# A recurrent attention and two-layer network kernel on one core: the first step and its network taken apart by batch, a new order of the first four steps, and one product that waits for the keys' transfers

## The chip, the core and the metric

The kernel runs on one core of a Trainium2 chip. The metric is the time of one execution on the device, in microseconds (us); less is better. The core has five engines with queues of their own: TensorE (PE; its weight loads are listed as PEld), VectorE (DVE), ScalarE (ACT), GpSimd (POOL) and SyncE (SP). SP, ACT and POOL also issue DMA transfers. An instruction waits on semaphores for what other engines or transfers must have done, and what stands behind it on its engine waits with it.

## What is computed

A gated recurrence over 768 positions (4 batches, 8 heads of 48), whose output is laid out as 3072 tokens of 384, and a two-layer network with a leaky activation:

```python
f = 1.0 / (1.0 + np.exp(-f_logit))
for t in range(S):
    state = f[:, :, t, :, None] * state + np.einsum('bhd,bhe->bhde', k[:, :, t], v[:, :, t])
    y[:, :, t] = np.einsum('bhd,bhde->bhe', q[:, :, t], state)
x = y.transpose(0, 2, 1, 3).reshape(B * S, H * D)
h = x @ w_in                                            # 384 -> 2048
g = np.maximum(h, 0.0) + alpha * np.minimum(h, 0.0)
out = g @ w_out                                         # 2048 -> 384
```

Inputs arrive in float32, the two weight matrices as 8-byte floats that the kernel turns into float32 itself.

## The kernel before

The work is cut into 12 steps: six chunks of 128 positions, and in each two pairs of batches (U = 2 batches a step, so 256 tokens). Steps 0 and 1 are the first chunk of the two pairs; they start from an empty state and use a shorter form of the diagonal blocks.

A step has four parts.

- *Preparation* (`prepare`, letter P, five pieces): loads of gates, queries, keys and values; the sigmoid on ScalarE; a chain of VectorE products that builds the decayed queries (`qd`, lags 1 to 3, lines 286 to 295), two scans of decays (317, 319), decayed keys (`k4`, `kh`, `ks`) and quads (`us`). From the second chunk on the keys are turned by VectorE (`kt`, line 401) and put in place by 16 small transfers from SP into `ksn` (line 427).
- *Carry* (`carry`, letter O, two pieces): the products between half chunks (`off`, line 444), in the first chunk also the half scores (454) and a turn of the keys by TensorE (`pk`, 471); then the new state (`pd`, line 484), which reads `ksn`, and its sum into `vs`.
- *Attention* (`attend`, letter S): for each batch raw scores (520) and quad scores (535), copied under masks into `ad` by VectorE; `ad` is copied by ScalarE into the score matrix `A` (563, eight copies of 32x256); the output product `py` (574), copied to `y`. Step 0 brings `y` into the layout `xT` by products with `dense` (592); the others do it by ten transfers on SP, ACT and POOL (603).
- *Network* (`network`, letter n): the first layer over 256 columns, eight tiles `ph` with two blocks of 128 hidden units each (618), a Relu on ScalarE (623), two gate instructions on VectorE (625). In step 0 the second layer is plain (`po`, 638). In the other steps it is seven half-size products `pa` to `pe` (657) with sums of gates (702).

The 16 weight pieces (letters a, w for the first matrix; b, v for the second) are loaded by SP into five raw buffers, converted by two ScalarE instructions each (224, 225), and put together by one VectorE instruction (234). W are differences of the second matrix that the seven products need.

The order of TensorE, VectorE and ScalarE is written out by hand as a string of these letters: `FIRST` for four steps, `USUAL` for every step from the fourth on. One letter runs one piece of a part, with all its instructions on all engines. POOL's and SP's instructions are placed by a scheduler. PSUM has two buffers of two banks (`psa`) for the attention and four single banks (`psn`) for the network. Before everything stand 52 small matmuls on constants (`idle`, line 736). In the usual order of TensorE a step reads: raw and quad of batch 0, first-layer tiles 0 and 1 of the step before, raw and quad of batch 1, tiles 2 and 3, off, state, tiles 4 to 7, pa, pb, output, pc, pd, pa, pc, pe.

Of the kernel before, what the change touches and what calls it, by code (L numbers as in the profile page):

```python
# [8 lines left out]
F32 = mybir.dt.float32  # L9
# [12 lines left out]
U = 2  # L22
# [4 lines left out]
IDLE = 52  # L27
# [3 lines left out]
FIRST = (  # L31
        "P5 a2 P a O w S w a w a2 S Q S O S w Q2 S Q2 S w",
        "a2 w2 n O b w n b2 S P v2 n2 S b v Q n b n O S2 v n b v n Q2 b v Q b n S v2 W Q W S n2 W n",
        "n S P n2 S W n W n O Q n3 O S Q n S Q n Q S2 Q n3",
        "S n3 P S Q S n O n O n4 Q S Q S Q n S Q n Q n2",
)
USUAL = "S n2 S n2 O2 n Q n3 Q n Q S3 n Q S n Q n Q n"

def flat(first, usual, steps=12):
    out = []  # L40
    left = {}
    for n in range(steps + 1):
        for key in (first[n] if n < len(first) else usual).split():
            for _ in range(int(key[1:] or 1)):
                k = key[0]
                if k in "awbvW":
                    out.append((k,))
                else:
                    m = n - 1 if k == "n" else n + 1 if k == "Q" else n
                    k = "P" if k == "Q" else k  # L50
                    if 0 <= m < steps:
                        out.append((k, m))
    return out

# [4 lines left out]
def kernel(  # L59
# [12 lines left out]

# [31 lines left out]
    psn = ctx.enter_context(tc.tile_pool(name="psn", bufs=4, space=bass.MemoryType.PSUM))  # L120

    def pair(name):
        return psa.tile([128, 2, 512], F32, tag="pair", name=name)

    def bank(name):
        return psn.tile([128, 512], F32, tag="net", name=name)
# [35 lines left out]
    nc.gpsimd.memset(mquad, 0.0)  # L162
    for m in range(1, NB):
        lo = UO[m] + (4 if m == 1 else 0)
        n = NB - m
        nc.gpsimd.tensor_copy(mquad[:, lo:lo + 4 * n].rearrange("p (i r) -> p i r", r=4),
                              inq[:, 0:n].unsqueeze(2).broadcast_to((128, n, 4)))
    mhalf = const.tile([128, VW], F32, tag="mhalf", name="mhalf")
    nc.gpsimd.memset(mhalf, 0.0)
    for half in range(2):  # L170
        for m in range(1, NQ):
            n = NQ - m
            lo = 16 * half + 4 if m == 1 else VO[m] + 4 * n * half
            nc.gpsimd.tensor_copy(mhalf[:, lo:lo + 4 * n].rearrange("p (i r) -> p i r", r=4),
                                  inq[:, NQ * half:NQ * half + n].unsqueeze(2).broadcast_to((128, n, 4)))
# [7 lines left out]
    make_identity(nc, ident)  # L183
    nc.gpsimd.tensor_scalar(om, om, -1.0, 1.0, ALU.mult, ALU.add)


    dense = work.tile([128, DM], F32, tag="o", name="dense")
    nc.gpsimd.memset(dense, 0.0)
    for par in range(2):
        nc.gpsimd.tensor_copy(dense[:, (2 + par) * D:(3 + par) * D], ident[:, 64 * par:64 * par + D])  # L190

    def load_weights(dst, src, name):

        rows_ = NK if dst is w_in_sb else 1
        pieces_ = dst.shape[1] * dst.shape[2] // WP
# [4 lines left out]
        got = {}  # L210

        def of(n):
            return dst[:, :, n * width:(n + 1) * width]
# [3 lines left out]

        def upper(n):
            raw = stage.tile([128, WP, 4], I16, tag="raw", name=f"{name}_raw{n}", bufs=RAWS)
            nc.sync.dma_start(out=raw.rearrange("p (a n) four -> p a (n four)", a=rows_)[:, :, 0:4 * width - 1],  # L220
                              in_=words[:, :, 4 * n * width + 1:4 * (n + 1) * width])

            lead = stage.tile([128, WP], F16, tag="lead", name=f"{name}_lead{n}", bufs=LEADS)
# [575 lines left out]
```

## Time and profile before

| What | Value |
|---|---|
| time, median of 3 runs | 621.4 us (621.33 to 623.4) |
| span of the profiled execution | 622.1 us |
| TensorE busy | 592.1 us, 95% |
| VectorE busy | 497.1 us, 80% |
| ScalarE busy | 246.6 us, 40% |
| POOL busy | 63.0 us, 10% |
| first-layer matmuls (L618) | 258.7 us in 1152 passes |

The profile shows one execution; its own time is known by its span alone, which is 0.7 us over the median of the runs. The span is cut there into 40 slices, with the busy share of each engine in tenths. Every float32 matmul shows as two passes, so a tile of six matmuls counts 12. Passes overlap: the mean of one is longer than the distance between the starts of two. The first real matmul starts at 17.8 us, the first-layer's first at 49.0 us, the first raw score of step 4 at 198.1 us; from there a step takes 47.7 us.

### The profile page before, as it was taken

To read this page: it belongs to the slowest core of one execution; us is meant where nothing else is said; L and a number is where in the kernel's file an instruction comes from. 1 tells how busy PE (TensorE), PEld (TensorE's weight loads), DVE (VectorE), ACT (ScalarE), POOL (GpSimd) and SP (SyncE) were. 2 spreads that over 40 slices of the span, in tenths; PEclk is the share of its full clock that TensorE was granted. 3 is DMA by queue.
4 is the path that set the end of the run, shared out by engine and by line. 5 is a ranking of instruction groups with operands and counts; after the bars stand their busy time and mean duration, and the time that the engine had idled before them with its cause. 6 is when DMAs were issued, how large, how long until landed. Compare 5 with 4: busy or idle time off the path is not lost.

```text
span 622.1 us, 19062 instructions
## 1 busy us (share of the span) xinstructions
PE 592.1 (95%) x8212; PEld 529.8 (85%) x8212; DVE 497.1 (80%) x997; ACT 246.6 (40%) x466; POOL 63.0 (10%) x117
## 2 busy tenths in 40 slices
PE   3568999999999999999999999999999999999997
PEld 3457866898899899899899899899889889889997
DVE  7588998899898798798798798798888888762261
ACT  5677862441641272262261351352253243223110
POOL 9120010001000011001001001001001000000000
PEclk9999999999999999999999999999999999999999
DMA  9964632014404314214313313413313401201000
GB/s 290 367 234 155 190 85 52 36 36 108 98 8 96 72 35 107 67 35 95 79 35 90 84 35 88 86 36 86 87 36 85 87 3 26 53 2 27 26 0 26
DMA packets 68116, 50.43 MB, mean 81 GB/s; under 512 B 47168, under 2 KB 60608, under 8 KB 68032
## 3 DMA queue, kind: packets, MB, share of 16 engines
q1 hardware_dynamic: 56656, 25.01, 15.6%
q0 software_dynamic: 6864, 22.35, 12.7%
q10 hardware_dynamic: 4512, 1.85, 1.7%
q8 instruction: 65, 1.06, 0.7%
q14 instruction: 19, 0.16, 0.1%
HBM read 36.21 MB, written 4.72 MB: 66 GB/s over the span
## 4 chain that ended last, share of the span: by engine, by line
PE 88%; DVE 6%; ACT 3%; issue 2%; DMA 1%; ACTq 0%; DVEq 0%
PE ph L618 39%; PE pc L657 9%; PE pa L657 8%; PE pd L657 5%; PE pe L657 4%; PE pb L657 4%; PE py L574 4%; PE po L638 3%; PE raw L520 3%; PE qu L535 3%; PE pd L484 3%; PE off L444 1%; PE xt L592 1%; DVE gate L625 1%; DMA f<-in_fT 1%
## 5 line engine op out<-in xcount | busy, mean ns | idle before, releaser
L618 PE MATMUL ph<-xT,w_in_sb 128*128 128x256 f32 x1152 | 258.7, 382 | 0.7 <-DVE Csum L661 0.7
L618 PEld LDWEIGHTS ph<-xT,w_in_sb 128*128 128x128 f32 x1152 | 216.4, 190 | 33.4 <-issue 2.3
L623 ACT ACTIVATE neg<-ph 128x512 f32<-128x512 f32 x96 | 57.4, 598 | 200.8 <-PE ph L618 139.5
L625 DVE SCALAR_TENSOR_TENSOR gate<-neg,om,ph 128x256 f32<-128x256 f32 x192 | 82.7, 478 | 50.6 <-ACT neg L623 50.4
L657 PE MATMUL pc<-t,S 128*128 128x192 f32 x352 | 61.7, 329 | 0.0
L657 PE MATMUL pa<-w_out_sb,gate 128*128 128x192 f32 x352 | 61.3, 327 | 0.1
L657 PEld LDWEIGHTS pa<-w_out_sb,gate 128*128 128x128 f32 x352 | 57.9, 190 | 1.0 <-DVE gate L625 0.4
L657 PEld LDWEIGHTS pc<-t,S 128*128 128x128 f32 x352 | 57.3, 190 | 0.6
L526 DVE COPY_PREDICATED ad<-mraw,raw 128x256 f32<-128x256 int32 (+1 forms) x96 | 42.4, 442 | 11.1 <-PE raw L520 8.6
L541 DVE COPY_PREDICATED ad<-mquad,qu 128x224 f32<-128x224 int32 (+6 forms) x140 | 42.0, 300 | 6.2
L419 ACT COPY A<-q 48x512 f32<-48x512 f32 x44 | 27.2, 619 | 36.1 <-DVE q L368 35.7
L563 ACT COPY A<-ad 32x256 f32<-32x256 f32 x96 | 38.7, 403 | 1.4
L330 DVE TENSOR_TENSOR us<-us,fs 128x768 f32<-128x768 f32 (+5 forms) x60 | 36.8, 614 | 0.0
L678 ACT ACTIVATE o<-pa 128x192 f32<-128x192 f32 x11 | 3.7, 332 | 75.2 <-PE pa L657 72.3
L661 DVE SCALAR_TENSOR_TENSOR Csum<-pc,Csum 128x192 f32<-128x192 f32 x22 | 7.9, 357 | 30.3 <-PE pc L657 30.1
L287 DVE TENSOR_TENSOR qd<-qd,f 128x768 f32<-128x768 f32 (+2 forms) x36 | 27.2, 756 | 6.0 <-ACT qd L282 6.0
L520 PEld LDWEIGHTS raw<-qd,k 48*32 48x32 f32 x1536 | 18.5, 109 | 15.3 <-issue 13.1
L520 PE MATMUL raw<-qd,k 48*32 48x80 f32 x1536 | 24.0, 243 | 7.6 <-issue 4.4
L702 DVE TENSOR_TENSOR S<-gate 128x512 f32<-128x512 f32 x44 | 30.3, 688 | 0.8
L657 PE MATMUL pe<-w_out_sb,S 128*128 128x192 f32 x176 | 30.4, 326 | 0.0
L657 PE MATMUL pd<-w_out_sb,S 128*128 128x192 f32 x176 | 30.4, 326 | 0.0
L657 PE MATMUL pb<-t,gate 128*128 128x192 f32 x176 | 30.4, 326 | 0.0
(101 smaller groups left out, 758.3 us busy)
## 6 DMA issues: line engine op xcount, KB each, us to landing
w_out_raw<-in_w_out SPq DMA_DIRECT2D x8, 767.8 KB, 5.8
w_in_raw<-in_w_in SPq DMA_DIRECT2D x8, 767.2 KB, 11.9
q<-in_qT POOLq DMA_DIRECT2D x11, 512.0 KB, 4.2
f<-in_fT POOLq DMA_DIRECT2D x11, 512.0 KB, 4.5
k<-in_kT POOLq DMA_DIRECT2D x11, 512.0 KB, 4.9
out<-o SPq DMA_DIRECT2D x24, 192.0 KB, 2.7
vs<-in_v POOLq DMA_DIRECT2D x22, 192.0 KB, 4.6
ksn<-kt SPq DMA_DIRECT2D x80, 32.0 KB, 2.0
```

Of the source, the lines that this page charges most:

```text
L287: nc.vector.tensor_tensor(qdv[d], qdv[d - 1][:, :, :, 1:5 - d], f[:, :, 1:5 - d].rearrange("p (g i) r -> p g i r", i=NB), ALU.mult)
L330: nc.vector.tensor_tensor(us[:, :, UO[m]:UO[m] + 4 * n].rearrange("p g (i r) -> p g i r", r=4), us[:, :, skip:skip + 4 * n].rearrange("p g ...
L419: nc.scalar.copy(A[halves(cc)[1], :, par * HP:(par + 1) * HP, CH * cc:CH * (cc + 1)], q3[rows(par)].rearrange("p (u h c) s t -> p u h c (s ...
L520: nc.tensor.matmul(raw[DB * j:DB * (j + 1), par, hp * C:hp * C + QW], lhsT=k[r_, g * DB:(g + 1) * DB], rhs=qd[r_, g], start=True, stop=True)
L526: nc.vector.copy_predicated(adu[:, :, :, d:4], mraw[:, d, :, d:4].bitcast(I32).unsqueeze(1).broadcast_to((128, H, NB, n)), rv[:, :, QO[d]: ...
L541: nc.vector.copy_predicated(ad[:, u, :, :, 4 * m:DB], mquad[:, lo:lo + n].bitcast(I32).unsqueeze(1).unsqueeze(1).broadcast_to((128, 2, HP, ...
L563: nc.scalar.copy(A[s_, u, :, s_], ad[s_, u].rearrange("p r h t -> p (r h) t"))
L618: nc.tensor.matmul(ph[:, j * T:(j + 1) * T], lhsT=w_in_sb[:, kt, m * 128:(m + 1) * 128], rhs=xT[:, kt], start=(kt == 0 and j == 0), stop=( ...
L623: nc.scalar.activation(neg, phv, AF.Relu, scale=-1.0)
L625: nc.vector.scalar_tensor_tensor(gate[:, m % NH, m // NH], neg[:, j], om[:, m:m + 1], phv[:, j], ALU.mult, ALU.add)
L657: nc.tensor.matmul(to[:, 0:DH], lhsT=of(f), rhs=by(f), start=(f == 0 and not more), stop=(f == NH - 1), skip_group_check=True)
L702: nc.vector.tensor_tensor(to, x_, y_, op)
```

## The change

The letters become words, one for a small piece of a part (a product, a copy, one VectorE group), and the order of the opening is written out anew, word by word, for everything up to step 4; POOL is now ordered by hand too. From step 4 on, the word order gives TensorE the same sequence as before, with one product more (`kw`). In particular:

- The 52 idle matmuls are gone.
- In step 0, loads, preparation, off, key turns, state and output are done for batch a (0) and batch b (1) apart: half-size instructions, twice as many.
- The first layer of step 0 runs by batch: groups of four blocks of 128 hidden units over 128 columns, 96 matmuls where 48 stood, one Relu of 128x512 a group and four gate instructions of 128x128.
- The half scores of steps 0 and 1 go into the free columns of `raw`; the quad scores of step 0 share one PSUM buffer. Step 0 has four more PSUM banks for its own use (`psf`) until the network's first bank is wanted.
- In the first chunk POOL, not ScalarE, copies the decayed queries into `A` (`s..`), and the copies of `ad` into `A` (`p..`) are spread over ScalarE (A), VectorE (V) and POOL (G): in step 0 all eight on POOL, in steps 1, 2 and 3 six, three and four.
- Three weight pieces are loaded from ACT's queue.
- `keys_landed` (word `kw`): a product of one column of the identity with four columns of `ksn` that all 16 transfers touch. It writes into the bank of first-layer tile 3, which then overwrites it. In the usual order it stands between tiles 2 and 3.
- In the usual order the turn of the keys (`ke`, `kt`) moves up on VectorE to directly behind `u2`, and ScalarE's four copies `c0` to `c3` ahead of the Relu of tile 5.

```diff
-USUAL = "S n2 S n2 O2 n Q n3 Q n Q S3 n Q S n Q n Q n"
+FIRST = """
+lda:0 ldb:0 id6V:0 id1V:0 id0V:0 id3V:0 qca:0 sga:0 kra:0 l1a:0 l2a:0 l3a:0 k4a:0 sgb:0 krb:0 qcb:0 c0b:0 l1b:0 l2b:0 l3b:0 scb:0 c3b:0 c0a:0 c2b:0
...
+fs:0 id2V:0 id4V:0 jd6V:0 id7V:0 jd2V:0 ih3:0 oc0a:0 oc1a:0 X0:0 s10a:0 p03G:0 p01G:0 s11b:0 il1:0 pdb:0 oc0b:0 bl:1 p02G:0 s11a:0 p00G:0 pda:0 m0a:0
+oc1b:0 c1:1 y0:0 z0A:0 t0:0 il5:0 m0b:0 ih5:0 T02A:0 X1:0 ib1:0 l2:1 ib3:0 k4:1 il2:0 l3:1 cg:1 T01A:0 ih2:0 c0:1 T00V:0 sc:1 p10G:0 p12G:0 s10b:0
+p11G:0 p13G:0 y1:0 ld:2 z1A:0 c3:1 na0:0 ih4:0 t1:0 T10A:0 c2:1 T11A:0 il4:0 ga0:0 r0:1 ib5:0 m1:0 jl6:0 T12A:0 ib2:0 nb0:0 le:1 sa:1 fs:1 gk:1 ib4:0
+sb:1 gb0:0 nb1:0 Ga0:0 nr:1 Gb0:0 h0:1 r1:1 h1:1 na1:0 H0:1 gb1:0 sg:2 jh2:0 jl1:0 ke:1 H1:1 R1:1 ib6:0 Gb1:0 nb2:0 na2:0 ga1:0 il7:0 qc:2 kr:2 jd0A:0
...
+USUAL = """
+r0 R0 x0 X0 n0- g0- G0- n1- g1- G1- r1 R1 x1 X1 n2- g2- G2- kw n3- g3- G3- S0- of oc0 oc1 pd m0 n4- g4- G4- ld+ sg+ kr+ qc+ l1+ l2+ l3+ c0+ c1+ c2+
+c3+ n5- g5- G5- n6- g6- G6- n7- g7- G7- S1- sc+ A1- B- ka- le+ k4+ e2+ p00A p01A p02A p03A p10A p11A p12A p13A y0 y1 C1- D- u2- ke+ kt+ e3+ e4+ sa+
+e5+ m1 z0A z1A mv A2- C2- d0- oa- e6+ km+ e7+ sb+ fs+ E- u3- b- d1- s00+ s01+ s10+ s11+ e-
...
+            def states(cc, par):
+                copy = nc.scalar.copy if c else nc.gpsimd.tensor_copy
+                copy(A[halves(cc)[1], u0:u1, par * HP:(par + 1) * HP, CH * cc:CH * (cc + 1)],
...
+        for mark, u0, u1 in (("a", 0, 1), ("b", 1, 2)) if n < SPLIT else (("", 0, U),):
+            part(mark, u0, u1)
...
+        def keys_landed():
+            to = ahead[n - 1, 3] = bank(f"phk_{i}")
+            nc.tensor.matmul(to[0:1, 0:4], lhsT=ident[:, 0:1], rhs=x["ksn"][:, 0, 0:128:32], start=True, stop=True,
+                             skip_group_check=True)
...
+        def put(u, j, engine):
+            s_ = slice(DB * j, DB * (j + 1))
+            copy = {"A": nc.scalar.copy, "V": nc.vector.tensor_copy, "G": nc.gpsimd.tensor_copy}[engine]
+            copy(A[s_, u, :, s_], ad[s_, u].rearrange("p r h t -> p (r h) t"))
...
+        def batch_first(u, g):
+            ph[u, g] = bank(f"ph{g}{u}_{i}")
+            for kt in range(NK):
+                for j in range(4):
+                    m = 4 * g + j
+                    nc.tensor.matmul(ph[u, g][:, j * C:(j + 1) * C], lhsT=w_in_sb[:, kt, m * 128:(m + 1) * 128],
+                                     rhs=x["T"][:, kt, u * C:(u + 1) * C], start=(kt == 0 and j == 0),
+                                     stop=(kt == NK - 1 and j == 3), skip_group_check=True)
...
-    with tc.manual_schedule(engines={mybir.EngineType.PE, mybir.EngineType.DVE, mybir.EngineType.Activation}):
-        for _ in range(IDLE):
-            nc.tensor.matmul(idle[0:32, 0:8], lhsT=ones[:, 0:32], rhs=ones[:, 0:8], start=True, stop=True)
+    with tc.manual_schedule(engines={mybir.EngineType.PE, mybir.EngineType.DVE, mybir.EngineType.Activation, mybir.EngineType.Pool}):
```

Words used below: `r0`, `r1` raw scores of a batch, `x0`, `x1` quad scores, `R`, `X` their masked copies, `h`, `H` half scores and their copies, `of` off, `kp` key turns, `pd` state, `y0`, `y1` output, `t0`, `t1` layout, `na0` to `nb3` first-layer groups of batch a and b, `ga0` and `Ga0` their Relu and gates, `n0` to `n7` first-layer tiles, `km` the 16 transfers of the keys. On TensorE the opening reads: r0, r1, kpb, h1, h0, x1, kpa, off, x0, pd, y0, t0, y1, na0, t1, then r0 of step 1, nb0, nb1, h0, r1, h1 of step 1, na1, nb2, na2, x1, of, x0, kp of step 1, na3, pd of step 1, nb3, y0 and y1 of step 1.

## The prediction

> **What bounds the kernel now.** I read the engine busy strips of the page first, then the busy time by stretches, then TensorE's waits and its timeline.
>
> ```profile
> PE   3568999999999999999999999999999999999997
> DVE  7588998899898798798798798798888888762261
> ```
>
> ```profile
> 0.00:60.40 60.40, 35.66 (x986) 30.89 (x986) 45.93 (x82) 40.46 (x71) 19.87 (x49) 1.00 0.78 261
> 60.40:198.10 137.70, 136.56 (x1770) 115.80 (x1770) 125.48 (x242) 64.24 (x117) 13.40 (x21) 1.00 0.32 83
> 198.10:532.00 333.90, 333.21 (x4593) 303.39 (x4592) 287.49 (x588) 125.24 (x246) 28.62 (x45) 1.00 0.28 64
> ```
>
> The columns are the stretch, its length and the busy time of PE, PEld, DVE, ACT and POOL. TensorE is the bound from 60.4 us on (136.6 of 137.7, 333.2 of 333.9). Time can be won in two places only: in the first 60 us, and where TensorE is busy but slow. VectorE is nearly full too (125.5 of 137.7), so what starts earlier on TensorE must also be ready earlier on VectorE.
>
> ```profile
> 43.73 5.46 PE L592 MATMUL xt<-y,dense 128*128 128x256 f32 x12 [1.71 <-ACT y L583]
> 48.98 3.15 PE L618 MATMUL ph<-xT,w_in_sb 128*128 128x256 f32 x12
> 54.85 1.09 PE L471 MATMUL pk<-ident,ks 128*128 128x128 f32 x8
> 60.54 0.81 PE L535 MATMUL qu<-us,k 48*32 48x52 f32 x64
> 74.33 5.45 PE L618 MATMUL ph<-xT,w_in_sb 128*128 128x256 f32 x24
> ```
>
> Each line has start and duration; the distance of two starts, by the count, is the price of one. A 256-column pass costs 224 ns (5.38/24; one matmul is two passes), but the 12 from 43.73 on cost 437 each: early on the array runs at half speed. At 60.54 TensorE has done step 0 up to one tile of its first layer and most of step 1's small products, worth at late prices: off 0.7, half scores 1.3, key turns 0.9, raw 1.4, quad 1.5, state 0.9, out 2.0, layout 2.7, two first-layer tiles 5.4, step 1's off, half, turns and raw 3.6: 20.4 us. So 40.1 us are lost by then, and 1.6 more by 198.1 (0.74 and 0.28 are its two longest waits).
>
> ```profile
> 119.28 0.76 PE L444 MATMUL off<-q,kh 48*32 48x32 f32 x64
> 119.97 8.04 PE L618 MATMUL ph<-xT,w_in_sb 128*128 128x256 f32 x36
> 127.93 0.94 PE L484 MATMUL pd<-vs,ksn 64*48 64x48 f32 x64
> 128.80 3.24 PE L657 MATMUL pa<-w_out_sb,gate 128*128 128x192 f32 x16
> ...
> 355.47 0.76 PE L444 MATMUL off<-q,kh 48*32 48x32 f32 x64
> 356.32 1.58 PE L484 MATMUL pd<-vs,ksn 64*48 64x48 f32 x64
> 357.84 10.63 PE L618 MATMUL ph<-xT,w_in_sb 128*128 128x256 f32 x48
> ```
>
> Here is the slow place. Off alone takes 0.69 and the state product 0.87 when it stands behind long matmuls; in steps 4 to 11 it stands behind off, whose 64 are gone in 0.7 us, and the pair takes 2.37 instead of 1.56. The program has 11 to 16 semaphore waits of the keys' transfers on its first matmuls.
>
> **The keys' product (steps 4 to 11).** It stands between first-layer tiles 2 and 3, behind 2.7 us of long matmuls, and takes over all waits on the keys' transfers. Removed: eight times 0.79, 6.3 us. Added: two passes of four columns, not shown in the trace. Lower bound: two passes of raw, 2 x 11 ns (0.69 us for 64). Upper: 0.79 each, if the waits show there. I take 0.1: in step 2 the same waits behind 36 long passes cost nothing (127.93 to 128.80). Net 5.5 us. Is the data there? The wait moves from 15.1 us into a step to about 11.7, and the key turn on VectorE moves up with it, to just behind the second-half sum, near 333.8 in the step that ends at 341.2, where it was done at 339.7. The 16 issues take 12 us on SP, landing is 2.0 us later: about 348, product at 352.9. Five us of cover; without the earlier turn it would be late by 2 us a step. Behind it wait only tile 3 and what follows. SP's result stores go behind the transfers; their tile is next wanted a step later. The other engines' order in these steps differs only in ScalarE's four quad copies moving ahead of tile 5's Relu; that gate is then ready near 368.4, and pa reads it at 369.5: nothing lost.
>
> **Idle matmuls.** They fill 2.1 to 7.8 us, ten before the first real one; removing them is free, since what ran from 17.8 to 49 us was slow with them.
>
> **The opening, followed queue by queue.** Half prices: a VectorE product of 1024, 512, 256 costs 1.12, 0.60, 0.34 between starts, so a split adds 0.08.
> 1. The first gate half has half of the 512 KB that landed in 4.0 us at 4.74; at the 385 GB/s of those slices about 4.1, the query half 4.8. ScalarE now copies queries first (0.55), and its order then has a second table load (1.28, the row of the first), then the sigmoid half 0.6: VectorE starts at 7.2, not 5.85.
> 2. VectorE then does what took 13.3 us (5.85 to 20.2 less a 1.0 wait), with 22 splits (1.8): 22.3. It goes on without the 6.2 us wait that it had: weight piece 0.95, raw copies 3.7, first lag of step 1 1.4, factors 0.35, quad copies 2.0: done at 30.7 (36.6 before).
> 3. The copies into A go to POOL. None is in the trace. Lower bound the mask copies, 0.2 each; upper the two dense copies below, 1.13. The sizes (32x256, 48x256) are nearer to neither; I take 0.8. From the first quad copies (29.7) six copies and two memsets (0.7) stand ahead of batch a's output: 35.2.
> 4. Output half at half speed 1.85, copy 0.54, layout 2.8 (12 x 0.23): 40.4. Batch b's output needs five more POOL copies (39.2): 42.2. First-layer group a0 starts there; tile 0 started at 48.98.
> 5. A group is 24 passes of 128 columns. Bounds: 112 ns (half of 224) and 190 (the mean weight load, if none overlapped: 14 us more in all). I take 116, from the key turns (0.93 for 8): 2.8 a group, 22.3 in all against 21.5, 0.8 dearer. a0, partly slow, 4.7; layout b 1.4; b0 must wait for the last layout copy, behind 2.9 us of ScalarE's queue: 51.3.
> 6. b0, b1, half scores and raw of step 1 (2.1), a1, b2, a2 (five groups, 14), quad, off, quad (2.2), first turns 0.5: 70.1. The rest of the turns needs the PSUM bank of a1, whose gates are 28.6 us of VectorE behind 40.7 and behind the quad product: 70.2. Turns 0.5, a3, state, b3, output (8.5): 79.2, and with some waits of the kind in 5 about 80.2.
>
> Work to there: 42.6. Lost: 37.6, against 41.7, less 1.6 of later waits that I keep and 0.9 of dearer work: 1.6 us won. SP issues ten loads for step 0 instead of five (0.5 to 0.7 each), so the first weight piece leaves near 7 us, not 4.0. The DMA engines are full until 30 us, the pieces land by that rate, and a0 wants its two at 42: no cost; without that cover it is 3 us of ScalarE's conversions.
>
> **Sum.** Profiled span 622.1, less 1.6, less 5.5: 615.0. The median of the runs, 621.4, is 0.7 below that span: 614.3, so **614**.
>
> **A rule on the early matmuls.** The Trainium skill (TensorE: Matmul & The Clock Gate, Part 1) says that the array starts at half clock and gets the full one after about 3.4 us of sustained work. The trace agrees on the two speeds (437 and 224 ns), but 5.2 us passed at the slow one from 43.73. By the rule a0 would cost 0.5 us less: 613.5.
>
> **Rivals.** *POOL's copies are held up behind VectorE (slower).*
>
> ```profile
> 11.91 1.19 DVE L321 TENSOR_TENSOR us<-us,f 128x1024 f32<-128x1024 f32 x1
> 13.03 1.24 DVE L347 TENSOR_TENSOR k<-k,kr 128x1024 f32<-128x1024 f32 x1
> 12.16 2.19 POOL L190 COPY dense<-ident 128x48 f32<-128x48 f32 x2
> ```
>
> Two copies of 48 elements took 1.1 us each, as long as the VectorE products beside them, while copies at 6.5 us, VectorE idle, took 0.2. At 1.13 plus 0.4 of its own (ScalarE's 32x256 copy takes 0.40) a copy costs 1.5: eleven ahead of batch b's output put it 6.5 later (29.7 + 0.7 + 16.5 + 1.85 = 48.8), and in step 1 eight more behind the quad copies (at 77.7) end at 90.2 where TensorE is ready at 84.8: 5.4. Sum 614 + 12 = 626. It eats the gain from about 1.25 us a copy, and is slower by over 0.5% from 1.4. Against it: many VectorE instructions there are shorter (0.44, 0.6).
> The Trainium skill (SBUF — State Buffer, Who interferes with whom) speaks for it: a VectorE instruction with two SBUF inputs and a GpSimd instruction that reads SBUF exclude each other for a whole instruction. The trace agrees (1.13 beside 1.12 to 1.24). By it VectorE is held too, 20 times 0.4, 8 us at most on an engine that has 12 us to spare before 198.
>
> *VectorE alone sets the opening (faster).* Its busy time to 198.1 is 171.4, 3.0 of it before its start; with 1.8 of splits, 1.7 of 32 gate instructions for 16 and 1.5 of copies moved to it, 173.4. From 7.2, with 4.1 for the layout, step 4 begins at 184.7: 198.1 less 13.4, span 603.2, time 602.5. For it: POOL near 0.2, and TensorE's waits covered. Against: it has no room for any wait.
>
> *The waits don't leave (no change).* If the keys' product shows its waits itself, only the opening is won: 619.8. Against it: step 2's state product.
>
> **How the numbers follow.** Forecast 0.5, VectorE alone 0.17, waits stay 0.13, POOL held 0.2. The forecast's own range is 609 to 619 (POOL at 0.2 wins 3 to 5, keys' product 0.03 to 0.4 moves 3). The range over the cases is 603 to 626. A measurement tells 0.5%, 3.1 us, from no change. Faster (below 618.3): 0.47 of the forecast, 0.17, 0.03 of the third: 0.67. Slower (over 624.5): 0.16 from POOL. Same: 0.17.
>
> **What would show it.** Off to first-layer tile in 1.6 instead of 2.37 in steps 4 to 11, 47.0 a step instead of 47.7. The first-layer's first 128-column pass near 42 us, 116 ns apart later. POOL copies near 0.8. First raw of step 4 at 196.5. Wrong if POOL's copies are over 1.25, if the keys' product has waits, if 128-column passes are near 190, or if VectorE, not TensorE, ends most waits between 50 and 190 us.

## The result and the profile after

| | median, us | executions | ratio to the kernel before, 95% |
|---|---|---|---|
| before | 622.62 | 20 (620.64 to 625.09) | |
| changed | 627.92 | 20 (621.50 to 636.53) | 1.0044 [1.0022, 1.0065] |
| forecast | 614 (603 to 626) | | |

The ratio leaves out the executions in which TensorE's clock was down for longest; they count in the median, and below it is shown that the kernel brings them about itself. The profiled execution took 633.04 us (span 631.3), one of the long ones: it is read here for what happens in it, and the sizes are taken from medians.

First the busy strips of the changed kernel's page and the granted clock in the same 40 slices:

```profile
PE   2479799999999999799999999999999999999997
DVE  7979989898799799489889879889889869762251
PEclk9999989999999999799999999999999999999999
```

Then its busy time by stretches. The columns are those of the same view before: stretch, length, PE, PEld, DVE, ACT, POOL, granted clock, DMA share and GB/s.

```profile
0.00:60.40 60.40, 35.30 (x974) 32.12 (x975) 49.98 (x113) 37.76 (x75) 26.66 (x62) 1.00 0.73 242
60.40:200.20 139.80, 134.17 (x1790) 114.58 (x1788) 128.12 (x248) 57.79 (x103) 22.06 (x33) 0.98 0.33 87
200.20:541.50 341.30, 333.68 (x4607) 301.21 (x4606) 289.69 (x595) 128.33 (x246) 29.62 (x47) 0.99 0.27 64
```

Step 4 starts at 200.2 us, not at the forecast 196.5 (198.1 before). VectorE did 4.0 us more in the first 60 us (49.98 against 45.93) and TensorE no more than before. From 200 on TensorE misses 7.6 us (341.30 less 333.68), where it missed 0.7, and its clock is below 1. The opening and the usual steps both need an explanation.

TensorE's timeline of the opening:

```profile
32.02 1.20 PE L610 MATMUL state<-vs,ksn 64*48 64x48 f32 x44 [5.12 <-issue]
35.74 1.98 PE L665 MATMUL py<-A,vs 128*64 128x64 f32 x32 [2.53 <-POOL A L651]
38.41 2.93 PE L688 MATMUL xt<-y,dense 128*128 128x128 f32 x12 [0.69 <-ACT y L674]
43.17 3.04 PE L752 MATMUL ph<-xT,w_in_sb 128*128 128x128 f32 x24
...
77.26 0.48 PE L665 MATMUL py<-A,vs 128*64 128x64 f32 x6 [1.99 <-POOL A L651]
78.61 3.46 PE L665 MATMUL py<-A,vs 128*64 128x64 f32 x58 [0.87 <-POOL A L424]
```

Up to the first 128-column passes this is the forecast (output at 35.2, passes at 42.2). Then the output product of step 1 waits for GpSimd's copies, and its 58 matmuls take 3.46 us: the clock is at 0.50 from 78 to 84 us.

Now a usual step without a stall, with the pair that the prediction was about:

```profile
211.77 0.19 PE L616 MATMUL phk<-ksn,ident 128*1 128x4 f32 x2
211.90 2.86 PE L734 MATMUL phk<-xT,w_in_sb 128*128 128x256 f32 x12
214.68 0.76 PE L587 MATMUL off<-q,kh 48*32 48x32 f32 x64
215.37 0.94 PE L610 MATMUL state<-vs,ksn 64*48 64x48 f32 x64
216.23 6.09 PE L734 MATMUL ph<-xT,w_in_sb 128*128 128x256 f32 x27
```

From off to the next tile 1.55 us (214.68 to 216.23) where it was 2.37: the waits did leave the state product. But here is the step that begins at 247.37:

```profile
256.30 2.86 PE L734 MATMUL ph<-xT,w_in_sb 128*128 128x256 f32 x12
263.59 0.19 PE L616 MATMUL phk<-ksn,ident 128*1 128x4 f32 x2 [4.43 <-DMA ksn<-kt]
263.71 5.30 PE L734 MATMUL phk<-xT,w_in_sb 128*128 128x256 f32 x12
268.94 0.76 PE L587 MATMUL off<-q,kh 48*32 48x32 f32 x64
```

The product of the keys waits 4.43 us for its transfers, and the tile behind it then takes 5.30 us instead of 2.86, at a granted clock of 0.50. The step takes 54.28 us. From 200.23 on the steps are 47.14, 54.28, 47.27, 48.49, 47.35, 47.33 and 49.41 us apart: four are 0.3 to 0.5 us shorter than before (47.63 to 47.78), and the three with a stall lose 10.3 us between them (against 47.3 each). In two of these three the product of the keys waits (4.43 us here, 2.14 in the step from 492.09 on). In the third, from 348.92 on, it doesn't: there the state product stops for 1.0 us between like matmuls, and nothing in the profile releases it.

```profile
364.07 0.74 PE L610 MATMUL state<-vs,ksn 64*48 64x48 f32 x44
365.82 0.47 PE L610 MATMUL state<-vs,ksn 64*48 64x48 f32 x20 [1.01 <-issue]
```

Why are the transfers of the keys late? SP's queue says it, in its list of waits (total, times, longest). The changed kernel, then the one before:

```profile
SPq L463 <- DMA xT<-y: 48.2, 22, 6.1
SPq L463 <- DVE kt L456: 32.5, 3, 18.5
```

```profile
SPq L427 <- DMA xT<-y: 37.7, 23, 4.4
SPq L427 <- DVE kt L401: 26.0, 10, 4.1
```

SP holds the keys' transfers (L463) until the layout moves of `y` have landed: `ksn` and `y` are two tiles under one tag with one buffer. Of the changed kernel's waits for the turn of the keys all but 0.8 us fall into the first four steps; from 190 us on SP waits 42.8 us for the moves. In the step of the stall the turn is done at 240.6 us, 6.8 before the step begins, and the transfers go out five us after that:

```profile
235.38 2.56 SPq L702 DMA_DIRECT2D xT<-y  x4
245.72 12.14 SPq L463 DMA_DIRECT2D ksn<-kt  x16
```

The 16 issues end at 257.9; the slowest data landed 7.0 us after its issue, while k and v of the next step (0.5 and 0.4 MB) were on their way.

### The profile page after: what moved, and what is told of

Read it like the earlier page. It is cut to its first block, busy times and chain, and to the rows that moved or that the text cites. A ratio compares the mean times of both kernels' runs of the same rounds, so it can differ in the third digit from the quotient of the medians.

```text
span 631.3 us, 19115 instructions
## 1 busy us (share of the span) xinstructions
PE 589.4 (93%) x8234; PEld 527.2 (84%) x8234; DVE 506.0 (80%) x1040; ACT 240.7 (38%) x455; POOL 79.4 (13%) x144
## 4 chain that ended last, share of the span: by engine, by line
PE 80%; DVE 8%; DMA 3%; issue 2%; SPq 2%; POOL 2%; ACT 2%; ACTq 0%; DVEq 0%; POOLq 0%
PE ph L734 31%; PE pa L830 9%; PE pc L830 8%; PE phk L734 4%; PE pb L830 4%; PE py L665 4%; PE pe L830 4%; PE pd L830 4%; PE po L794 3%; PE qu L509 2%; PE raw L488 2%; DVE ut L320 2%; SPq L463 2%; PE state L610 1%; DMA xT<-y 1%
## 5 line engine op out<-in xcount | busy, mean ns | idle before, releaser
L734 PE MATMUL ph<-xT,w_in_sb 128*128 128x256 f32 x948 | 213.2, 382 | 0.3 <-issue 0.3
L734 PEld LDWEIGHTS ph<-xT,w_in_sb 128*128 128x128 f32 x948 | 177.7, 190 | 27.3 <-issue 2.6
L740 ACT ACTIVATE neg<-ph 128x512 f32<-128x512 f32 x79 | 46.5, 598 | 146.0 <-PE ph L734 111.7
L744 DVE SCALAR_TENSOR_TENSOR gate<-neg,om,ph 128x256 f32<-128x256 f32 x158 | 67.8, 477 | 38.2 <-ACT neg L740 36.4
L496 DVE COPY_PREDICATED ad<-mraw,raw 128x256 f32<-128x256 int32 (+1 forms) x96 | 42.2, 442 | 3.1 <-PE raw L488 0.6
L702 POOL DMA_DIRECT2D xT<-y x22 | 11.8, 541 | 259.6 <-ACT y L674 259.6
L424 ACT COPY A<-q 48x512 f32<-48x512 f32 x40 | 24.7, 617 | 51.3 <-DVE q L320 51.0
L320 DVE TENSOR_TENSOR ut<-ut,fs 128x128 f32<-128x128 f32 (+5 forms) x75 | 41.3, 554 | 1.0
L340 ACT COPY ut<-qd 128x256 f32<-128x256 f32 (+1 forms) x52 | 31.7, 631 | 13.0 <-DVE qd L320 12.7
L665 PE MATMUL py<-A,vs 128*64 128x64 f32 x768 | 29.4, 239 | 5.4 <-POOL A L651 4.5
L665 PEld LDWEIGHTS py<-A,vs 128*64 128x64 f32 x768 | 27.1, 151 | 8.6 <-POOL A L651 4.9
L651 ACT COPY A<-ad 32x256 f32<-32x256 f32 x73 | 29.2, 401 | 6.4 <-DVE ad L517 5.3
```

Source lines behind the costliest of these rows:

```text
L320: nc.vector.tensor_tensor(a, b, of, ALU.mult)
L340: w[f"c{r}{mark}"] = lambda r=r: nc.scalar.copy(q4()[:, gs, :, r], qdv[r][:, gs, :, 0])
L496: nc.vector.copy_predicated(adu[:, :, :, d:4], mraw[:, d, :, d:4].bitcast(I32).unsqueeze(1).broadcast_to((128, H, NB, n_)), rv[:, :, QO[d] ...
L651: copy(A[s_, u, :, s_], ad[s_, u].rearrange("p r h t -> p (r h) t"))
L665: nc.tensor.matmul(to[64 * par:64 * par + 64, u, o:o + CH], lhsT=vs[bp][:, cc, u, hd * D:hd * D + 64], rhs=A[:, u, par * HP + hp, CH * cc: ...
L734: nc.tensor.matmul(ph[f][:, j * T:(j + 1) * T], lhsT=w_in_sb[:, kt, m * 128:(m + 1) * 128], rhs=x["T"][:, kt], start=(kt == 0 and j == 0), ...
```

## The experiments

Theories, as the expectations name them. **A**: the keys' transfers wait for the layout moves (one buffer), the product of the keys then waits, and a stall of some us also halves TensorE's clock; a second loss of its own is step 1's wait for GpSimd. **B**: only the first steps cost. **C**: the clock falls without a wait. **D**: the product pays as forecast. **E**: the execution profiled before was long in its opening. **F** and **G**: VectorE does or doesn't set the end of the opening.

**1. `y` in a buffer of its own.** The buffer of the query input is free from its copy into `qd` until the next load, so `y` can have it.

```diff
-                x["y"] = work.tile([128, U, HP, C], F32, tag="ksn", name=f"y_{i}", bufs=1)
+                x["y"] = work.tile([128, U, HP, C], F32, tag="q" if n >= 3 else "ksn", name=f"y_{i}", bufs=1)
```

> The attention output y takes the buffer of the query input q instead of the one of the transposed keys, from step 3 on; everything else is the changed kernel. Theory A (the keys' transfers start only when the layout moves that read y have landed, because both tiles share one buffer; the column product of the keys then waits, and a wait of two to four us also halves the granted clock of TensorE for some us): the transfers of steps 5 to 10 start 5.5 to 7 us before their step's first raw product instead of 1.7 to 3.8, the column product waits nowhere, all steps 4 to 11 take 47.1 to 47.4 us, the granted clock falls nowhere behind 200 us, and the median is 620 to 623 with a spread below 6 us, against 628 and 15. Theory B (the first steps are what costs: copies on GpSimd in step 1, and a halved clock at 78 to 84 us): the transfers start earlier, but the median stays at 626 to 629 and the spread near 15. Theory C (the clock is taken down without any wait behind it): half clock behind 200 us stays as often as before.

Measured: 623.07 us (12 executions, 620.73 to 625.23; ratio 1.0023 [1.0011, 1.0035]). The transfers of the usual steps, here those of the step from 341.10 on, start 6.7 us ahead of it, and from 190 us on SP waits in front of them for the turn alone (8 times, 21.3 us):

```profile
329.77 1.88 SPq L702 DMA_DIRECT2D xT<-y  x3
334.38 11.65 SPq L463 DMA_DIRECT2D ksn<-kt  x16
```

The product of the keys waits nowhere, all distances from step 4 on are 47.19 to 47.44 us, and the spread falls from 15 to 4.5 us. B and C fall for the usual steps: in its profile the clock is 1.00 throughout. The median is just above the upper end of what A expected.

**2. The other way to it: loads in another order.** Layout moves that are issued beside 1 MB of loads of f and q land late. With k in front, which waits for the raw products, GpSimd's queue holds f and q back.

```diff
-                for name, src in (("f", fT), ("q", qT), ("k", kT)):
+                for name, src in (("f", fT), ("q", qT), ("k", kT)) if n < 5 else (("k", kT), ("f", fT), ("q", qT)):
```

> From step 5 on the loads of a step are issued with k ahead of f and q, nothing else; k waits for the raw products of the step before, so f and q (0.5 MB each) leave GpSimd's queue some 20 us later, behind the layout moves of y instead of beside them. Theory A with contention as the cause of the late landing: the layout moves land 2.0 to 2.6 us after their issue, as those of step 10 do, where no load runs beside them, instead of 4 to 7; the keys' transfers start 5 to 6.7 us before their step's first raw product, the column product waits nowhere, median 620 to 623, spread under 6 us, the same as with a buffer of its own. If the loads are not what holds the moves: starts at 2 to 4 us as now and 628. If f then comes late: ScalarE's sigmoid waits for it and each of steps 4 to 10 is some us longer, over 632.

Measured: 622.40 us (621.12 to 625.93; ratio 1.0019 [1.0004, 1.0034]). The changed kernel's transfers around 340 us, with the median time from issue to landing in the last column:

```profile
f<-in_fT POOLq DMA_DIRECT2D x1, 512.0 KB, 4.8
q<-in_qT POOLq DMA_DIRECT2D x1, 512.0 KB, 6.0
xT<-y SPq DMA_DIRECT2D x3, 48.0 KB, 4.7
xT<-y ACTq DMA_DIRECT2D x3, 48.0 KB, 4.2
```

With k in front the moves of the same step land in:

```profile
DMA to landing us min/median/max: 2.0/2.1/2.6
```

So the buffer makes the transfers wait for the moves, and the loads make the moves late. Breaking either link is enough: the transfers start 5.9 to 6.7 us ahead of their steps, the product of the keys waits nowhere, and ScalarE's sigmoid waits for nothing. The Trainium skill (DMA: Bandwidth & Descriptors, section "Issuing engines are not separate DMA queues") says that transfers from SP, ScalarE and GpSimd run on the same 16 DMA engines and interleave; the trace agrees for the moves of SP and ScalarE, with 2.1 us for 16 KB without the loads and 4.7 and 4.2 beside loads that GpSimd had issued. The two moves of GpSimd's own queue landed in 2.1 beside them.

**3. The product taken out.**

```diff
-r0 R0 x0 X0 n0- g0- G0- n1- g1- G1- r1 R1 x1 X1 n2- g2- G2- kw n3- g3- G3- S0- of oc0 oc1 pd m0 n4- g4- G4- ld+ sg+ kr+ qc+ l1+ l2+ l3+ c0+ c1+ c2+
+r0 R0 x0 X0 n0- g0- G0- n1- g1- G1- r1 R1 x1 X1 n2- g2- G2- n3- g3- G3- S0- of oc0 oc1 pd m0 n4- g4- G4- ld+ sg+ kr+ qc+ l1+ l2+ l3+ c0+ c1+ c2+
```

> The column product of the keys is taken out of steps 4 to 11, nothing else. Theory A: the wait for the keys' transfers falls back on the state product, 3 us later, so that stalls become rare and short (under 1.5 us each); the step from the off-diagonal product to the first layer's tile is 2.3 us again instead of 1.55, a step takes 47.7 to 48.0 us, and the median is 623 to 627 with a spread of 3 to 8 us. Theory D (the column product pays as forecast, and the loss lies elsewhere): about 8 x 0.7 = 5.5 us slower than the changed kernel, 632 to 635, with the same spread of 15 us.

Measured: 625.70 us (5 executions, 624.16 to 626.50), the steps 47.55 to 47.82. D falls: the changed kernel as it stands has a median of 627.92 in one set of executions and of 624.63 in another (yardsticks, below), so its product of the keys is worth about nothing; what it wins in quiet steps its own waits take. With this edit on top of experiment 1 it is seen alone:

> y in the query input's buffer from step 3 on, as in the first experiment, and the column product of the keys taken out of steps 4 to 11. Tells what the product itself is worth where its data is there in time. Theory A: the wait-free product wins 0.43 us a step (0.80 off the pair, less 0.33 for itself with the break that it makes between two tiles, less 0.14 on the first product behind tile 7), so 3 to 3.5 us: without it 626 to 627, against 623.1 with it, and steps of 47.6 to 47.8. Forecast's size (0.69 a step): 628 to 629. If the buffer alone is what helps and the product nothing: 623.

Measured: 627.12 us (6 executions, 625.14 to 629.64; ratio 1.0085 [1.0062, 1.0107]) against 623.07 with the product: it is worth 4.0 us where its data is there. It also tells the price of the opening: the steps of this kernel are those of before (47.56 to 47.89), and yet it is 5.3 us slower than the kernel before beside it (621.85). Its step 4 starts at 200.7 us.

**4. The product in the kernel before.** One column product of `ksn` into the bank of tile 3, with the old opening and the old order; then the same with `y` in the query buffer.

```diff
             tiles = (2 * f, 2 * f + 1) if plain else (f, f + NH)
+            if f == 3 and 3 <= steps.index((bp, c)) < len(steps) - 1:
+                nc.tensor.matmul(ph[0:1, 0:4], lhsT=ident[:, 0:1], rhs=latest["ksn"][:, 0, 0:128:32], start=True, stop=True,
+                                 skip_group_check=True)
```

> The kernel before, with one addition: in steps 4 to 11 a column product of the transposed keys ahead of the first layer's tile 3, as in the changed kernel; its opening and its order stay. There the transfers start 1.5 us before the step. Theory A (the transfers' start is set by the layout moves and their 14 us length, so a product 11.7 us into the step comes before they have landed): the product waits about 2 us in each of steps 4 to 10, the clock halves in some, the median is 628 to 645 against 621.8. Theory D (the product pays as forecast): 621.8 less 8 x 0.43 = 618.4.

> The kernel before with the same column product, and with y in the query input's buffer from step 3 on, so that the transfers wait for the keys' turn alone. Its opening is that of the kernel before. If the turn there ends late enough to hold the transfers (it ends 1.5 us before the step), the product still waits 2 us a step: over 628. If the layout moves held them as well by the same time, the same. If the turn is early enough: 618.4.

Measured: 636.88 us (ratio 1.0251 [1.0234, 1.0268]), and with the other buffer 639.15 (1.0257 [1.0234, 1.0280]). The first one's timeline in the step that begins at 346.46:

```profile
355.37 2.86 PE L623 MATMUL ph<-xT,w_in_sb 128*128 128x256 f32 x12
360.28 0.19 PE L619 MATMUL ph<-ksn,ident 128*1 128x4 f32 x2 [2.05 <-DMA out<-o]
360.40 4.54 PE L623 MATMUL ph<-xT,w_in_sb 128*128 128x256 f32 x12
```

Its granted clock (the number before the last two) right behind the wait:

```profile
360.00:361.00 1.00, 0.72 (x4) 0.63 (x5) 0.24 (x1) 0.00 (x0) 0.00 (x0) 0.92 0.00 2
361.00:362.00 1.00, 1.00 (x4) 0.79 (x3) 0.00 (x0) 0.00 (x0) 0.00 (x0) 0.50 0.07 16
...
364.00:365.00 1.00, 1.00 (x18) 0.63 (x19) 0.00 (x0) 0.00 (x0) 0.00 (x0) 0.88 0.00 0
```

The profile names a store that was issued behind the transfers; the product itself reads `ksn` alone, and its weight load waits for `ksn<-kt`. It is a wait of 2 us as forecast for this case, and 1.7 us more for the tile behind it (4.54 for 2.86): that makes steps of 49 to 51.5 us, from the second of them on. The buffer alone doesn't help there, because in that order the turn itself ends late (SP's wait for `kt` grows from 24.7 to 44.5 us). So the earlier turn is needed, and with it the other buffer or the later loads of experiment 2; the change brought the turn alone.

**5. Step 1's copies off GpSimd.**

```diff
-jh1:0 k4:2 jb0:0 jb1:0 jd5V:0 c1:2 jl3:0 jl2:0 jb2:0 p02A:1 p10G:1 p03G:1 p01G:1 p12G:1 s10:1 p00G:1 p13A:1 m0:1 jh5:0 c3:2 gb3:0 jl5:0 jh3:0 s11:1
-p11G:1 y0:1 y1:1
+jh1:0 k4:2 jb0:0 jb1:0 jd5V:0 c1:2 jl3:0 jl2:0 jb2:0 p02A:1 p10G:1 p03A:1 p01G:1 p12A:1 s10:1 p00A:1 p13A:1 m0:1 jh5:0 c3:2 gb3:0 jl5:0 jh3:0 s11:1
+y0:1 y1:1
```

(and `p11V:1` behind `X0:1`)

> Four of the six 32x256 copies of step 1's attention matrix that GpSimd makes go to other engines (three to ScalarE, one to VectorE ahead of the scans of step 2), nothing else. Theory A: GpSimd is done near 76 instead of 79.7 us, the output product of step 1 waits under 1 us for it instead of 2.9 and runs at full clock, y of step 1 ends at 78 to 80 instead of 82.0, the first raw product of step 4 comes at 195 to 198 instead of 200.2; the median falls by 2 to 5 us to 623 to 626, and the spread stays above 8 us, since the keys' waits stay. Theory B: the median falls to 621 to 623 and the spread to under 6 us. If ScalarE and VectorE are the bound there, the time stays at 628.

Measured: 622.57 us (619.42 to 630.44; ratio 1.0010 [0.9988, 1.0032]). The changed kernel's GpSimd in step 1:

```profile
70.67 0.39 POOL L651 COPY A<-ad 32x256 f32<-32x256 f32 x1 [12.85 <-DVE ad L533]
...
75.83 1.38 POOL L651 COPY A<-ad 32x256 f32<-32x256 f32 x1
77.26 1.29 POOL L424 COPY A<-q 48x512 f32<-48x512 f32 x1
78.62 1.07 POOL L651 COPY A<-ad 32x256 f32<-32x256 f32 x1
```

The copies end at 79.7 us, where TensorE is free at 75.3. With the edit GpSimd is done at 76.0, but the output product now waits 1.1 us for ScalarE's state. Step 4 starts at 198.5. The median is B's, the spread of 11 us is A's; the two edits together decide:

> The changed kernel with y in the query input's buffer from step 1 on, and with the four copies of step 1's attention matrix moved from GpSimd to ScalarE and VectorE: the two edits that each took about 5 us off. Theory A (two independent losses: the keys' waits, and step 1's wait for GpSimd): spread of the first edit (under 6 us), T of step 4's first raw product 196 to 198.5, steps of 47.2 to 47.4 us; median 619 to 621. Rival (both edits only remove the same chance of a halved clock): the median stays at 622 to 623.

Measured: 621.00 us (619.48 to 622.83; ratio 0.9992 [0.9979, 1.0004]). Against 624.63 for the changed kernel (yardsticks, below) the two edits win 1.6 and 2.1 us apart and 3.6 together: the losses add up, and both go. A's figure for step 4 was wrong, though: it starts at 199.8 in this execution, so something else still holds the opening.

**6. Yardsticks.**

> The kernel before, unedited, profiled once more as a yardstick for the opening. Its profiled execution of 622.1 us span lay about 2 us above the median of its runs (a run's time is 1.75 us more than its span, so the median of 621.8 is a span of 620.0). Theory E (the opening of that execution was slow by those 2 us): the first raw product of step 4 comes at 195.5 to 197 instead of 198.1, so that the changed kernel's 199.2 to 200.2 is 3 to 4 us of loss in the opening and not 1 to 2. Rival: it comes at 198 and the 2 us lie elsewhere.

> The changed kernel, unedited, beside the experiments as their yardstick. If its loss is steady and not one of the chip it ran on: median 626 to 630 with a spread over 10 us, ratio to before 1.003 to 1.012, and the first raw product of step 4 at 199 to 200.5 us. If the five us that single edits took off were only another chip's: a median near 622 to 623.

The kernel before, profiled again: 622.90 us, step 4 at 197.55, between the two expectations' figures. Its usual steps vary by 0.2 us, so where an execution is shorter, its opening is; the median execution of the runs beside it (621.51) would start step 4 near 196.2 (197.55 less the difference of 1.39, an estimate). The changed kernel again: 624.63 us (12 executions, 622.15 to 632.11; ratio 1.0049 [1.0021, 1.0076]), step 4 at 199.85. The ratio is the same as in the first 20 executions. The median is 3.3 us lower and lies between the two that were expected: 3 of 12 executions took over 628 us, against 10 of 20. Whether that is chance or the chip that it ran on isn't shown.

**7. What sets the rest of the opening.** All copies of steps 0 and 1 into `A`, states too, on ScalarE, on top of `both`:

> Both edits, and all copies of steps 0 and 1 into the attention matrix taken from GpSimd to ScalarE, the two states of these steps too. Theory A (GpSimd's copies hold VectorE's products up, 128x1024 at 1.40 to 1.56 beside them and 1.12 to 1.23 else, and set the start of step 0's output): VectorE's busy time of the first 199 us falls from 178 to 175 or 176, the output of step 0 starts at 34 to 35.5 instead of 36, step 4 starts at 196.5 to 198.5, median 618.5 to 620.5 against 621.0. Rival (ScalarE with its weight pieces is as late as GpSimd was): step 4 stays at 198.5 to 200, median 621 to 623.

Measured: 631.99 us (4 executions, 630.81 to 632.86), a miss of both figures by over 8. ScalarE, in order, reaches the copies too late (4.4 us in step 0, the rest in step 1):

```profile
PE py L665 <- ACT A L651: 5.2, 2, 4.4
...
PE py L665 <- ACT A L424: 3.9, 1, 3.9
```

In this order GpSimd is the better engine for step 0. In step 1 the place in ScalarE's order is what can be bettered: `p02A:1 p10G:1 p03A:1 m0:1 p01G:1 p12A:1 s10:1 p00A:1 p13A:1` moved ahead of `jh1:0 k4:2 jb0:0 jb1:0 jd5V:0 c1:2 jl3:0 jl2:0 jb2:0`.

> Both edits, and in step 1 ScalarE's copies of the state and of the attention matrix stand ahead of four weight pieces of the output layer and of step 2's query copy. Theory A: the output product of step 1 waits for nothing behind tile b3 (now 1.1 us of waits), y of step 1 ends at 78.5 to 80, step 4 starts at 197 to 198.5, median 619 to 621. Rival (VectorE and the weight pieces set the opening, what is won here is waited for at the output layer of step 0): the first output products wait 1 to 3 us for their weights, and the median stays at 620.5 to 622.5.

Measured: 620.51 us (619.45 to 623.71; ratio 0.9976 [0.9962, 0.9989]), step 4 at 198.4. This is the one version that beats both kernels, by 1.3 and 4.1 us at the medians. TensorE's timeline shows what comes next in the queue:

```profile
73.60 2.94 PE L752 MATMUL ph<-xT,w_in_sb 128*128 128x128 f32 x24
76.48 2.08 PE L665 MATMUL py<-A,vs 128*64 128x64 f32 x64
79.75 2.82 PE L794 MATMUL po<-w_out_sb,gate 128*128 128x384 f32 x8 [1.18 <-DVE w_out_sb L241]
83.20 2.82 PE L794 MATMUL po<-w_out_sb,gate 128*128 128x384 f32 x8 [0.63 <-DVE gate L764]
```

The output product waits no more; the second layer now waits for VectorE. The same stretch of 30 us, by engines, in the kernel before (second profile) and in this one:

```profile
50.00:80.00 30.00, 28.82 (x618) 24.45 (x617) 26.75 (x52) 26.78 (x47) 1.45 (x2) 1.00 0.53 169
```

```profile
50.00:80.00 30.00, 27.35 (x688) 26.29 (x687) 29.16 (x68) 20.10 (x37) 6.10 (x9) 1.00 0.51 157
```

TensorE is busy for 1.5 us less, VectorE for 29.16 of 30. Two kernels put a known load on it, and as much on ScalarE:

```diff
+    def more():
+        for _ in range(4):
+            nc.vector.tensor_copy(mquad, mquad)
+
+    pieces["zz"] = more
```

(`zz:0` ahead of `l1:2`, `l3:2` and `k4:2`; for ScalarE five times `nc.scalar.copy(lvl, lvl)`)

> The kernel of the last experiment with VectorE given 3.6 us more to do in step 1: at three places between 66 and 78 us four copies of a constant onto itself (128x224, about 0.3 us each). Theory F (VectorE, busy 29.4 of 30 us between 50 and 80, sets the end of the opening): step 4 starts 2.5 to 3.6 us later than 198.4, median 623 to 624.2 against 620.5. Theory G (TensorE or ScalarE sets it, VectorE has room): under 1 us, 620 to 621.5.

> The same kernel with ScalarE given about as much more instead: at the same three places five copies of a 128x64 constant onto itself (about 0.23 us each, 3.5 us in all). Theory F: ScalarE is busy 20 of 30 us there, so step 4 starts under 1.5 us later, median 620.5 to 622. If ScalarE's order sets the opening: 2.5 to 3.5 us later, 623 to 624.

Measured: 623.56 us (622.07 to 628.37) with 3.5 us more on VectorE, 3.1 later at the median, which is F's size. With 3.7 us more on ScalarE 622.52 (620.69 to 624.53), 2.0 later, more than F gave it and less than its rival. Step 4 starts at 202.87 and 198.87 in the two profiles, 4.4 and 0.4 us later; the first of these executions took 2.8 us more than its median, the second 0.4 less. But neither delay is the added work alone. In each profile a wait of TensorE is about 2 us long, and the clock is at 0.50 behind it, from 71 to 74 and from 83 to 86 us:

```profile
70.16 4.54 PE L758 MATMUL ph<-xT,w_in_sb 128*128 128x128 f32 x24 [1.89 <-ACT A L599]
```

```profile
82.52 4.51 PE L800 MATMUL po<-w_out_sb,gate 128*128 128x384 f32 x8 [2.16 <-DVE gate L770]
```

Without the load the waits there are 1.36 and 0.63 us, the groups take 2.92 and 2.82, and the clock stays at 1.00; so 1.6 and 1.7 us of the delays are clock. The two runs show that more work on either engine can lengthen a wait of TensorE here. How much of a delay VectorE's work makes by itself, they don't show.

## Why the prediction failed, step by step

In terms of medians the sum comes apart like this. The opening stands by `buffer_no_product` against the kernel before, the product by `y_own_buffer` against that, and the waits by the changed kernel (two sets of executions) against `y_own_buffer`.

| term | forecast, us | measured, us |
|---|---|---|
| opening | -1.6 | +5.3 |
| keys' product, its data there | -5.5 | -4.0 |
| waits of the keys' product | 0 ("Five us of cover") | +1.6 to +4.9 |
| sum | -7.1 | +2.8 to +5.3 |

The rows add up to within 0.9 us only, as the kernels ran beside different sets of the kernel before (621.5 to 622.6). Two steps of the forecast failed: in the usual steps its "Five us of cover", and in the opening, the larger miss of 6.9 us, the sum that let TensorE run on from step 1's output with "some waits" of a us and the "1.6 of later waits" of the kernel before.

- **The pair off and state.** Right: 1.55 us forecast as 1.56.
- **The product's own cost, 0.1 us.** Mis-sized. The product takes 0.12 us, but it also parts two first-layer tiles, which then take 2.79 us each instead of 2.69 (5.70 with the product against 5.37). So 0.33 of the 0.80 go and 0.47 is left, which the steps' lengths bear out (47.29 us on average with the product and 47.75 without, `y` in its own buffer in both).
- **"Nothing lost" by the new order of ScalarE's copies.** Mis-sized by 0.14 us a step: the first `pa` behind tile 7 takes 2.74 us between starts instead of 2.60, with the product (`y_own_buffer`) and without it (`buffer_no_product`). In one step of each of these profiles, the gates of tiles 5 to 7 wait 1.14 us for ScalarE's Relu (0.31 before), and the last weight loads of `pa` wait 0.2 us for a gate, which they don't in the profile before.
- **"Five us of cover."** This is the step that failed in the usual steps. The turn did move up, to 6.8 us ahead of the step, about where the forecast put it. The forecast let the transfers follow it at once. They stood behind another semaphore, the landing of the layout moves, which the profile before shows in SP's list of waits with 23 entries, 37.7 us in all. The start moved from 1.5 to only 1.7 to 3.8 us ahead of most steps; with 11 to 12 us of issues and 2 to 7 us to landing, a product 12 us into the step is on the edge. Experiments 1, 2 and 4 show each link. The forecast had also left the landing at 2.0 us. That is still the median, but the slowest of a step's sixteen took 3.2 to 7.0 us, and 5.0 and 7.0 in the two steps where the product waits.
- **The opening up to step 1's output.** Nearly right: output of batch a at 35.74 (35.2), first 128-column passes at 43.17 (42.2) and 120 to 115 ns apart (116), b0 at 48.33 (51.3), GpSimd's 20 copies 0.79 us on average (0.8). Idle matmuls: their removal shows nowhere, a0 ran at full speed at once (3.04 us, 4.7 forecast). That b0 came 3.0 us early was luck: nothing in the forecast gave it. (The granted clock reads 1.00 in the first 60 us of both kernels, so the slow passes there are known by their distances alone.)
- **GpSimd in step 1.** The forecast charged these copies in the rival alone, at 1.5 us each, and left "some waits" of about a us in its own sum. They end 4.4 us after TensorE is free (79.7 and 75.3). The eight copies of this step took 0.93 us on average; at 0.8 each the seven behind the last quad copies would still end near 78.1, so their place did more than their price. Moving four of them and the state's copy is worth 2.6 us (623.07 to 620.51). The executions' mean clocks suggest that much of this is the clock: the four of experiment 1's kernel with 0.999 or more have a median of 621.55 us, the eight others 623.91; with the copies moved (`both`) all twelve are at 0.999 or more.
- **Behind step 1's output.** The forecast followed TensorE past step 1 as if its queue were the only one. In `y_own_buffer`'s profile, with the clock at 1.00 throughout, step 1's output ends at 80.8 us (80.2 forecast, thanks to the early b0), but step 4 starts at 199.2 (196.5). So 2.1 of these 2.7 us are lost behind that output, and most of them between 115 and 165 us, where TensorE waits 2.6 us and in the kernel before (second profile) 0.9:

```profile
115.00:165.00 50.00, 47.43 (x532) 42.31 (x531) 44.92 (x87) 14.97 (x29) 5.50 (x9) 1.00 0.25 61
```

```profile
115.00:165.00 50.00, 49.15 (x726) 44.08 (x724) 46.34 (x95) 19.78 (x38) 4.47 (x7) 1.00 0.29 74
```

- **VectorE.** "VectorE alone" was a rival on the faster side, with 173.4 us of work. In the changed order VectorE has 175 to 176 us of work by 197 us, against 171.3 before, and is busy for 29.2 to 29.4 of 30 us between 50 and 80. That it sets the rest of the opening is argued, not shown. In `state_first` 4.0 of TensorE's 4.9 us of waits from 40 to 205 us end with VectorE; in `y_own_buffer` it is 2.0 of 7.1, while 2.9 end with GpSimd and 2.2 have no name. `more_vector` has the size for it, but with the clock in it. What causes the 2 us or so that `state_first` still loses in the opening (step 4 at 198.4, near 196.2 before by estimate) stays open.
- **Profile and median.** The forecast set the profiled span, 622.1 us, beside the median time, 621.4, as if both were one measure. A run's time is 1.75 us more than its span, so the execution profiled before was 1.2 to 2.3 us longer than the medians of 621.5 to 622.6, and that lay in its opening (step 4 at 198.1, near 196.2 at the median by estimate). A gain reckoned against that opening was too large by as much.
- **No term for a halved clock.** A stall was costed at its own length. It can cost half as much again, or nearly twice that: 4.43 us of wait and 2.44 for the tile behind it, in `before_product` 2.05 and 1.68, in `more_vector` 1.89 and 1.62.

## What to carry to other kernels

When a producer is moved earlier, look in the queue's own list of waits for everything that its consumer's issue waits for: a buffer shared under one tag is a dependency that no reading of the two instructions shows. A stall on TensorE of about two us or more can be paid one and a half times to nearly twice, so a wait that is moved to an earlier place without certain cover can cost more than the clean steps win. And a path followed on one engine holds only as far as the other engines have room: here one of them was busy for 29.4 of 30 us. Before a gain is summed up, the profiled execution must be placed among the runs: here it was one of the longer ones.

## What was not expected of the hardware

**The clock falls after short stalls, and not always.** In `before_product` a wait of 2.05 us between two tiles was followed by 3 us at 0.50, from 361 us on, when the matmuls were already running again. In the changed kernel the stall of 4.43 us brought 0.50 from about 262 to 268.7, that is until 5.1 us after work had come back. But the wait of 2.14 us at 505.9 in the same execution changed nothing, and the 3 us of waits in step 1 brought 0.50 from 78 to 84 us in the changed kernel's profile and none in that of `y_own_buffer`, with the same waits (1.98 and 0.90). The Trainium skill (TensorE: Matmul & The Clock Gate, Part 1) gives an idle window of about 3.4 us that runs freely, so that the moment differs from run to run. The trace agrees on the two speeds and on the chance; here the clock was back 3.5 to 5.8 us after the last wait. That 2.05 us can be enough, and 1.89 in `more_vector`, is shorter than the page's figure.

**Copies on GpSimd lengthen VectorE's work, and seem to be lengthened by it.** The same 32x256 copy took 0.39 us when it came first (70.67) and 1.07 to 1.38 a few us later beside other VectorE instructions. VectorE's pieces of the output weights (128x768) took 1.14 us on average in `y_own_buffer` and 1.04 in the kernel before, and a product of 128x1024 1.40. With the copies taken from GpSimd (`no_gpsimd_copies`) the same two took 1.04 and 1.23.

**A wait without a name.** In step 0 the state product stops for about 5 us between two like matmuls (32.02, "issue") in every profile of the changed order, 4.3 to 5.4 us, always behind the 20th of its 64 matmuls. The DMA engines are full there (a share of 0.9 to 1.1), and nothing in the profile releases it. It cost nothing in the kernels whose copies GpSimd makes, since those end later. But a stop of the same kind cost 1.2 us in the usual step from 348.92 on, and one of 0.67 us lengthened a step of `k_loaded_first`. That it comes behind the same matmul each time speaks for a cause tied to that place in the program; what it is stays open.
